# Gradient stage of a recurrent attention: rows' gradient for x rows only, 20 full row tiles, and transposes moved from TensorE to the DMA crossbar

## The chip, the cores and the metric

One core of one Trainium2 chip runs the whole program. The metric is the device time of one execution in microseconds, read for several executions. The profile is one execution with the hardware profiler on. Before the change the time is 5564.06 us (median of 3 runs, 5560.69 to 5575.1).

## The reference, cut to what matters

```python
def _A_ref(x, mem0, Wq, Wk, Wv, Wo, seg_len):       # x: (1, 2048, 640) bf16, after a layernorm
    ...                                              # H = 32 heads, Dh = 128, M = 8, seg_len = 32
    mem = mem0
    for s in range(n_seg):                           # 64 segments, one after the other
        xs = x[:, s * seg_len:(s + 1) * seg_len, :]
        h = jnp.concatenate([mem, xs], axis=1)       # 8 memory rows + 32 x rows
        q = jnp.einsum('btd,dhe->bhte', h, Wq)       # k and v alike
        ...
        p = _softmax(scores, axis=-1)
        o = jnp.einsum('bhqk,bhke->bhqe', p, v)
        o = jnp.einsum('bhte,hed->btd', o, Wo)
        mem = o[:, :M, :]
        outs.append(o[:, M:, :])
    return jnp.concatenate(outs, axis=1)
# out = x + _A_ref(xn) * silu(B_ref(xn)); returned: out and the gradients
# with respect to x, mem0, Wq, Wk, Wv, Wo, w1, w3, w2
```

The change concerns one stage of the backward pass. It has, in memory, the softmax probabilities P and the scores' gradient dS, and the rows of q, k and of the outputs' gradient. For each tile of 3 segments (96 x rows and 24 memory rows, 120 in all; 22 tiles cover 64 segments, the last with one segment) and for each four heads (512 columns; eight such groups) it makes the rows' gradients of v, k and q. From these come the gradients of Wv, Wk and Wq (a product over rows with the rows h) and the gradient of the rows of h (a product over columns with the weights).

## The kernel before

The stage, cut to the parts that the argument touches. `nc.tensor` is TensorE, `nc.sync` the queue of SyncE (SP), `nc.scalar` ScalarE (ACT), `nc.gpsimd` GpSimd (POOL), `nc.vector` VectorE (DVE). A "unit" is one tile of rows in one group of four heads.

```python
def ld(u):                                   # loads of one unit
    nc.sync.dma_start(dS[0:n, :, 0:n], k.DSR[tl][:, h0:h0 + 4, :])
    nc.sync.dma_start(Pr[0:n, :, 0:n], k.PR[tl][:, h0:h0 + 4, :])
    for nm_ in ("g", "q", "k"):
        ...
        k.load_x(r, nm, src, nc.scalar if nm_ == "g" else nc.sync)
        k.load_m(r, tl, nm_, c0, c0 + 512, nc.gpsimd)

def s1(u):                                   # turn dS on TensorE
    for j in range(4):
        nc.tensor.transpose(pt[:, j, :], dS[0:n, j, :], k.ident[0:n, 0:n])
    nc.vector.tensor_copy(dST[0:n, :, 0:n], pt[0:n])

def s2(u, i):                                # rows' gradient i: P, dS or turned dS times rows
    for j in range(4):
        nc.tensor.matmul(pr[:, j * P:(j + 1) * P], lh[0:n, j, :], rh[0:n, j * P:(j + 1) * P], start=True, stop=True)
    ...                                      # PSUM to gr: ACT, DVE, ACT for i = 0, 1, 2

def s3(u, i0, i1):                           # turn the gradients on TensorE, copy into a ring
    for i in range(i0, i1):
        for j in range(4):
            nc.tensor.transpose(pt[:, i - i0, j, :], st["g", u, i][0:n, j * P:(j + 1) * P], k.ident[0:n, 0:n])
    ...
    k.copy(ring[:, i0:i1, :, d0:d0 + p1 - p0], pt[:, :, :, p0:p1], eng='s' if c == 2 else 'v')

def s4(u):                                   # turned gradients times weights, windows of 128 rows
    for w in range((120 * tl) // P, (120 * tl + n) // P):
        for h in range(2):
            for i in range(3):
                for j in range(4):
                    nc.tensor.matmul(pg[:], ring[:, i, j, r0:r0 + P], Ws[qd][i][:, j, 320 * h:320 * h + 320], ...)
        ...                                  # DVE adds pg to the accumulator

def wg(qd, i):                               # weight gradient i of the group: 22 tiles x 5 products
    for tl in range(NTL):
        for dc in range(DC):
            nc.tensor.matmul(accs[dc][:], hr[0:n, tl, dc * P:(dc + 1) * P], st["g", NTL * qd + tl, i][0:n, :], ...)
    for dc in range(DC):
        ot = io.tile([P, 512], BF16, name="wgo", tag="wgo", bufs=4)
        k.copy(ot[:], accs[dc][:], eng='vs'[dc % 2])
        nc.sync.dma_start(outf[2 - i][dc * P:(dc + 1) * P, c0:c0 + 512], ot[:])

for qd in range(8):
    for tl in range(NTL):                    # "unit part": ld(u+4), s2(u+2), s1(u+3), s3(u+1), s4(u)
        ...
    ...                                      # weights and first three units of the next group are loaded
    for i in range(3):                       # "product part"
        wg(qd, i)
        if qd < 7:
            next(h)                          # first steps of the next group
```

## Time and profile before

| kernel before | value |
|---|---|
| median of 3 runs | 5564.06 us |
| span and mean granted TensorE clock of the profiled run | 5562.0 us, 0.952 |
| unit part / product part / whole group, mean of the last seven groups, from the starts of the products (a group is counted from one product part to the next, so the two parts do not quite add up to it) | 107.5 / 78.3 / 186.7 us |
| first unit part, from the first product | 120 us |

From the page of the kernel before: busy time of each engine in us (share of the span) and its instructions; then the busy tenths of TensorE in 40 equal slices, and the share of the DMA engines likewise.
```profile
PE 4935.7 (89%) x66673; PEld 3152.5 (57%) x67020; DVE 2343.2 (42%) x7398; ACT 1783.4 (32%) x4953; POOL 1570.4 (28%) x2604
...
PE   4987888888888677989999997999999999998999
...
DMA  7553455555555686666666666354335433657332
```
A slice is 139 us, so the stage lies in slices 25 to 36, and slices 26 to 35 are wholly in it. There TensorE stands at 9, and DMA between 3 and 6.

### The profile page before, as it was taken

To read this page: it belongs to the slowest core of one execution; us is meant where nothing else is said; L and a number is where in the kernel's file an instruction comes from. 1 tells how busy PE (TensorE), PEld (TensorE's weight loads), DVE (VectorE), ACT (ScalarE), POOL (GpSimd) and SP (SyncE) were. 2 spreads that over 40 slices of the span, in tenths; PEclk is the share of its full clock that TensorE was granted. 3 is DMA by queue.
4 is the path that set the end of the run, shared out by engine and by line. 5 is a ranking of instruction groups with operands and counts; after the bars stand their busy time and mean duration, and the time that the engine had idled before them with its cause. 6 is when DMAs were issued, how large, how long until landed. Compare 5 with 4: busy or idle time off the path is not lost. (4 is left out here: it accounts for less than half of the span.)

```text
span 5562.0 us, 164947 instructions
## 1 busy us (share of the span) xinstructions
PE 4935.7 (89%) x66673; PEld 3152.5 (57%) x67020; DVE 2343.2 (42%) x7398; ACT 1783.4 (32%) x4953; POOL 1570.4 (28%) x2604
## 2 busy tenths in 40 slices
PE   4987888888888677989999997999999999998999
PEld 2554555555555444656666665566556655666665
DVE  5833555555555323444444542233223322311451
ACT  2422555555555322323333332233113312300111
POOL 0000344444444212333333333243224322310000
PEclk9998999999999778999999998999999999999999
DMA  7553455555555686666666666354335433657332
GB/s 252 171 185 90 137 152 153 158 156 162 153 151 143 152 171 155 176 186 184 186 184 178 185 169 130 76 124 99 94 74 126 98 87 83 162 166 188 106 117 92
DMA packets 1126617, 808.27 MB, mean 145 GB/s; under 512 B 672971, under 2 KB 1016679, under 8 KB 1123179
## 3 DMA queue, kind: packets, MB, share of 16 engines
q1 hardware_dynamic: 884995, 555.06, 37.3%
q0 software_dynamic: 91472, 144.46, 9.3%
q10 hardware_dynamic: 149388, 98.17, 6.3%
q8 instruction: 529, 8.67, 0.7%
q14 instruction: 233, 1.91, 0.1%
HBM read 468.47 MB, written 296.78 MB: 138 GB/s over the span
## 5 line engine op out<-in xcount | busy, mean ns | idle before, releaser
L1403 PE MATMUL wg<-gr,hr 120*128 120x512 bf16 (+1 forms) x2640 | 592.9, 386 | 17.3 <-DVE dST L1335 13.1
L1381 PE MATMUL g<-w,gT 128*128 128x320 bf16 x3840 | 548.4, 299 | 0.0
L1403 PEld LDWEIGHTS <-hr 120*128 120x128 bf16 (+1 forms) x2640 | 258.9, 99 | 343.1 <-issue 52.1
L1381 PEld LDWEIGHTS <-gT 128*128 128x128 bf16 x3840 | 368.8, 98 | 136.3
L243 POOL DMA_DIRECT2D r<-GOS x256 | 143.4, 564 | 795.8 <-PE r6p L1345 704.8
L90 DVE CAST wgo<-wg 128x512 bf16<-128x512 f32 x72 | 47.5, 688 | 589.2 <-issue 281.8
L316 PEld LDWEIGHTS <-hx 128*32 128x32 bf16 x7680 | 179.7, 97 | 169.4 <-issue 12.4
L90 DVE CAST stg<-bank 128x512 bf16<-128x512 f32 x256 | 177.0, 692 | 208.4 <-PE bank L316 199.4
L335 PEld LDWEIGHTS <-gkv 128*8 128x8 bf16 x8192 | 189.7, 87 | 107.4 <-DVE gkv L1012 23.8
L619 ACT ACTIVATE xP<-xsp,xnm 120x120 bf16<-120x120 f32 (+1 forms) x704 | 240.5, 376 | 8.5 <-DVE xnm L615 4.5
L1390 DVE TENSOR_TENSOR ghacc<-ghacc,g 128x320 f32<-128x320 f32 x240 | 117.0, 487 | 277.7 <-PE g L1381 277.7
L92 ACT CAST wgo<-wg 128x512 bf16<-128x512 f32 x48 | 25.8, 589 | 640.3 <-PE wg L1403 640.3
L1163 POOL DMA_DIRECT2D DSR<-gdS x176 | 101.6, 577 | 426.5 <-DVE gdS L1161 383.3
L1348 ACT CAST gr<-r6p 120x512 bf16<-120x512 f32 (+1 forms) x176 | 103.3, 587 | 361.7 <-PE r6p L1345 340.8
L668 POOL DMA_DIRECT2D OR<-xv x163 | 94.6, 580 | 418.9 <-ACT xv L667 287.0
L92 ACT COPY gT<-t6g 128x960 bf16<-128x960 bf16 (+5 forms) x216 | 167.0, 792 | 119.9 <-PE t6g L1364 117.0
L630 POOL TENSOR_TENSOR xP<-xP,xrz 120x480 bf16<-120x480 bf16 x163 | 161.8, 992 | 141.0 <-ACT xP L619 96.5
L1161 DVE SCALAR_TENSOR_TENSOR gdS<-gdp,Dx,gPr 120x120 bf16<-120x120 f32 (+1 forms) x680 | 182.7, 330 | 0.0
L1232 PE MATMUL gbank<-WqT,ident 128*128 128x512 bf16 x453 | 159.5, 402 | 20.1 <-issue 12.2
L335 PE MATMUL bank<-Wo,oTm 128*32 128x320 bf16 x4032 | 177.0, 329 | 0.1
L316 PE MATMUL gbank<-WoT,gox 128*32 128x512 bf16 x2560 | 153.6, 387 | 24.6 <-POOL gox L967 21.2
L1364 PE MATMUL t6g<-ident,gr 120*128 120x120 bf16 (+1 forms) x2112 | 172.0, 221 | 3.3 <-DVE wgo L90 2.7
(339 smaller groups left out, 10991.0 us busy)
## 6 DMA issues: line engine op xcount, KB each, us to landing
QVS<-stg SPq DMA_DIRECT2D x128, 256.0 KB
gqv<-QVS SPq DMA_DIRECT2D x108, 192.0 KB
vTt<-VTD SPq DMA_DIRECT2D x64, 320.0 KB
VTD<-gvT POOLq DMA_DIRECT2D x168, 120.0 KB, 3.6
OR<-xv POOLq DMA_DIRECT2D x163, 120.0 KB, 2.5
DSR<-gdS POOLq DMA_DIRECT2D x168, 112.5 KB, 3.4
dS<-DSR SPq DMA_DIRECT2D x168, 112.5 KB
P<-PR SPq DMA_DIRECT2D x168, 112.5 KB
```

Source lines behind the costliest of these rows:

```text
L90: return nc.vector.tensor_copy(out, in_)
L92: return nc.scalar.copy(out, in_)
L243: eng.dma_start(d, src if src.shape[0] > 1 else src[0])
L316: k.nc.tensor.matmul(bank[32 * g:32 * g + 32, :], x[:, dc, :], W[:, dc, c0:c0 + 512], start=(dc == 0), stop=(dc == k.DC - 1), tile_positio ...
L335: k.nc.tensor.matmul(pm[p0:p0 + nq, 0:320], x[:, h, :], W[:, h, 320 * b:320 * b + 320], start=(first and i == 0), stop=(last and i == 15), ...
L619: nc.scalar.activation(Pb[0:n, j, 0:n], sp[0:n, j, :], ACT.Exp, bias=nmx[0:n, j:j + 1], scale=k.scale, accum_out=Z[0:n, j:j + 1])
L630: eng.tensor_tensor(Pb[0:n, :, 0:n], Pb[0:n, :, 0:n], bc_last(rz[0:n], n), ALU.mult)
L1161: nc.vector.scalar_tensor_tensor(dS[0:n, j, :], dp[0:n, j, :], Dx[0:n, j:j + 1], Pr[0:n, j, :], op0=ALU.subtract, op1=ALU.mult)
L1232: nc.tensor.matmul((bA if g in ("W1", "G1", "G2") else bB)[:], k.ident[:], WqT[:, 0, 0:512], start=True, stop=True)
L1364: nc.tensor.transpose(pt[:, i - i0, j, :], st["g", u, i][0:n, j * P:(j + 1) * P], k.ident[0:n, 0:n])
L1381: nc.tensor.matmul(pg[:], ring[:, i, j, r0:r0 + P], Ws[qd][i][:, j, 320 * h:320 * h + 320], start=(i == 0 and j == 0), stop=(i == 2 and j ...
L1403: nc.tensor.matmul(accs[dc][:], hr[0:n, tl, dc * P:(dc + 1) * P], st["g", NTL * qd + tl, i][0:n, :], start=(tl == 0), stop=(tl == NTL - 1))
```

## The change

The intent is to take work from TensorE, which bounds the stage. (1) The gradient of h is made for x rows only, as the memory rows' one isn't used: x rows now come first in a tile, so that 16 windows of 128 rows stand in for 20. (2) Two of the 22 tiles are handled first, written to memory, and read back into the eight free partitions of the 20 others, so that the weight gradients need 20 tiles of 128 rows. (3) dS and the gradients are turned by two crossbar transposes of the DMA per unit, issued by SP, in place of sixteen TensorE transposes and three copies. (4) The loads of x rows are all issued by ScalarE; the loads of dS and P become contiguous; five buffers replace three.

The core of the diff, with cuts; the rest changes the layout of the tiles elsewhere (x rows first).
```diff
-            nc.sync.dma_start(dS[0:n, :, 0:n], k.DSR[tl][:, h0:h0 + 4, :])
-            nc.sync.dma_start(Pr[0:n, :, 0:n], k.PR[tl][:, h0:h0 + 4, :])
+            nc.sync.dma_start(dS[0:n], k.DSR[tl][:, h0:h0 + 4, :])
+            nc.sync.dma_start(Pr[0:n], k.PR[tl][:, h0:h0 + 4, :])
 ...
-                k.load_x(r, nm, src, nc.scalar if nm_ == "g" else nc.sync)
+                k.load_x(r, 0, src, nc.scalar)
 ...
+        def dturn(u):
+            dST = io.tile([P, 4, P], BF16, name="dST6", tag="dST6", bufs=4)
+            turned_load(k, dST[:], st["l", u][0][:].rearrange("p j c -> p (j c)"))   # SP: DMA transpose
 ...
+            g3 = gra[:, tl] if tl < NF else gp.tile([120, 3, 512], BF16, name="grs", tag="grs", bufs=2)[:]
 ...
+            if tl >= NF:
+                nc.gpsimd.dma_start(k.GSP[qd, r0:r0 + n], g3[0:n])
+
+        def spill(qd):
+            nc.gpsimd.dma_start(gra[120:P], k.GSP[qd].rearrange("(t r) i c -> r t i c", r=8))
 ...
-                    nc.tensor.transpose(pt[:, i - i0, j, :], st["g", u, i][0:n, j * P:(j + 1) * P], k.ident[0:n, 0:n])
+            turned_load(k, ring[:, :, a:a + nx], st.pop(("g", u))[0:nx].rearrange("p i c -> p (i c)"))
 ...
-            for tl in range(NTL):
-                n = k.geo(tl)[3]
+            for tl in range(NF):                     # NF = 20
 ...
+            for p in range(NTL):
+                u = u0 + p
+                if p + 3 < NTL:
+                    s2(u + 3)
+                    ld_to(u + 3 + NB)                # NB = 5
+                dturn(u + 4)
+                if p + 2 < NTL:
+                    s3(u + 2)
                 s4(u)
+                if p == 4:
+                    spill(qd)
```

## The prediction

> **What bounds the kernel now.** I read the page first (TensorE busy 89% of the span, at 8 or 9 tenths in nearly every slice, so the kernel is bound by TensorE almost everywhere), then the source lines of the changed stage in the view of one line's instructions, which says when each starts. The weight gradient stage runs from 3410 us (first transpose of dS) to 4915 us (last product), 1505 us. It handles eight groups of four heads. In each a "unit part" makes the rows' gradients of 22 row tiles, turns them and multiplies them with the weights (22 iterations), and a "product part" forms the weight gradients from all 22 tiles. The busy times by window, for the second group's two parts and the whole stage (columns: window, length, busy us and instructions of PE, PEld, DVE, ACT, POOL, then granted clock, DMA share, GB/s):
> ```profile
> 3610.00:3719.00 109.00, 103.29 (x1081) 81.34 (x1080) 50.91 (x113) 44.53 (x71) 55.84 (x101) 0.97 0.53 124
> 3719.00:3797.00 78.00, 74.00 (x351) 33.32 (x350) 6.16 (x11) 3.23 (x6) 1.70 (x3) 0.98 0.27 60
> 3410.00:4915.00 1505.00, 1414.16 (x11408) 916.27 (x11408) 458.14 (x992) 382.68 (x616) 457.64 (x828) 0.96 0.43 103
> ```
> One group takes 109 + 78 = 187 us, and eight of them 1496 us. TensorE is busy 94% of it; the transfers are at half share in the unit part and a quarter in the product part. Everything but TensorE has slack. The groups of instructions in the stage say what fills TensorE:
> ```profile
> L1403 PE MATMUL wg<-gr,hr 120*128 120x512 bf16 x2520 | 564.6, 386 | 17.3 <-DVE dST L1335 13.1 <-DVE gr L1350 2.6 <-DVE ghacc L1388 0.6
> L1381 PE MATMUL g<-w,gT 128*128 128x320 bf16 x3840 | 548.4, 299 | 0.0
> L1364 PE MATMUL t6g<-ident,gr 120*128 120x120 bf16 x2016 | 168.3, 223 | 3.3 <-DVE wgo L90 2.7 <-ACT wgo L92 0.5
> L1333 PE MATMUL t<-ident,dS 120*128 120x120 bf16 x672 | 67.4, 227 | 42.7 <-DMA dS<-DSR 39.0 <-DVE wgo L90 2.1 <-DVE gr L1350 0.8
> ```
> The reader is to see that the idle time (third field) is near zero, and that transposes by TensorE (L1364, L1333) are a real part of the load. Durations overlap in the pipeline, so one instruction's cost comes from the starts in the timeline of one iteration:
> ```profile
> 3663.45 0.37 PE L1333 MATMUL t<-ident,dS 120*128 120x120 bf16 x4
> 3663.66 0.58 PE L1364 MATMUL t6g<-ident,gr 120*128 120x120 bf16 x8
> 3664.08 0.39 PE L1345 MATMUL r6p<-r,dST 120*128 120x128 bf16 x4
> 3664.30 0.37 PE L1364 MATMUL t6g<-ident,gr 120*128 120x120 bf16 x4
> 3664.51 3.42 PE L1381 MATMUL g<-w,gT 128*128 128x320 bf16 x24
> 3667.78 0.39 PE L1345 MATMUL r6p<-r,P 120*128 120x128 bf16 x4
> ```
> Four small ones pass every 0.21 to 0.22 us (55 ns each), and 24 of 320 columns in 3.27 us (136 ns each). A weight product costs 592.9 us / 2640 = 225 ns, from the page.
>
> [...] from 3420 to 3428 us, where the three weight transposes run nearly alone, 242 GB/s move at a DMA share of 1.16.
> ```profile
> 3420.00:3428.00 8.00, 0.04 (x1) 0.00 (x0) 0.00 (x0) 0.60 (x1) 0.56 (x1) 0.50 1.16 242
> 3630.00:3690.00 60.00, 60.00 (x660) 48.56 (x658) 30.84 (x70) 26.84 (x43) 32.70 (x59) 1.00 0.60 142
> L280 SPq DMA_TRANSPOSE w<-in_A_Wv_dram x8: 2285/2478/3046, 3418.6 to 4652.2; - x8
> L280 SPq DMA_TRANSPOSE x<-in_B_w_dram x4: 1210/4666/15807, 5091.1 to 5117.4; - x4
> ```
> I use the measured rate. No transpose in this trace has SBUF as its source, as all the new ones do.
>
> **The change, part by part.** Removed from TensorE: all turns of dS (704) and of the gradients (2112), 2816 x 55 ns = 155 us. Rows' gradients for x rows only: 16 windows of 128 rows in place of 20, so 8 x 4 x 24 = 768 matmuls x 136 ns = 105 us. Twenty full tiles of 128 rows in place of 22 of 120 (the two leftover tiles, 160 rows, go through memory into the eight free partitions of each of the 20): 240 x 225 ns = 54 us. Sum **314 us**, all on the path, as TensorE has no other work to do there. If nothing else came to bind, the stage would take 1191 us and the kernel 5250.
>
> Also removed, off the path: DVE's 176 copies of turned dS (0.4 us) and the copies of turned gradients by ACT and DVE (about 0.96 and 0.41 us per unit). DVE and ACT are under half busy, so this gains nothing directly.
>
> Added, per unit: a crossbar transpose of dS, 128 x 512 elements (131 KB), and one of the three gradients, 96 x 1536 (295 KB), both on SP's queue. Moved: q and k loads from SP to ACT. The dS and P rows become 1024 contiguous bytes in place of four of 240; the packet records give 73 ns for 1024 bytes and 18 for 240, the same rate, so I book no gain.
>
> New TensorE time of a group: unit part 19 x 12 x 55 ns (three units' worth moves to the product part) + 16 windows x 3.27 = 12.5 + 52.3 = 65 us; product part 300 x 225 ns + 3 x 0.66 = 69.5 us. Now the other resources in the unit part:
> - Transfers. 19 units are loaded there (five buffers let the others go ahead). A unit's loads are 5 x 123 = 614 KB: 11.7 MB. Transposes: 22 x 131 + 20 x 295 KB = 8.8 MB. Output rows and the leftover tiles' reads and writes: about 1.8 MB. Sum 22.3 MB. The second row above gives 142 GB/s at share 0.60, 237 GB/s at full share: **94 us**, against 65 of TensorE.
> - SP's issue. A transpose of 640 rows x 128 took at least 1.21 us to issue, one of 640 x 512 about 2.4: a line through these gives 1.14 us for the dS one and 1.51 for the gradients' (estimates). With two plain issues of 0.45 us: 3.55 us x 19 + 2.65 x 3 = **75 us**, without waits.
> - The loop through SP. The built program issues a unit's dS and P loads when TensorE has freed their buffer, then the dS transpose for the next step, which TensorE needs one iteration later. Issue of both loads 0.9 us, of the transpose 1.1, landing some 2 us behind its queue, the last product 0.3: about 4.3 us, x 22 = **95 us**. And every transfer of SP and ACT waits for the one eight issues before, seven per unit, so about one unit's transfers are in flight.
>
> So the stage turns from TensorE-bound to transfer-bound in its unit part: I take 95 us, and 69 for the product part, whose transfers (outputs, next weights, three units' loads, near 30 us) are hidden. A group falls from 187 to 164 us, eight save 184; 5 us back for a start that waits on more loads before the first product. **5564 - 179 = 5385 us.** Outside the stage only layouts change (x rows first, memory rows last), with the same instruction counts; I book nothing.
>
> **The rivals.**
> (a) TensorE stays the bound: transposes out of SBUF run faster than those out of HBM[...]. For: stores out of SBUF in the packet records run at some 20 GB/s per engine against 14 for loads. Against: three limits of 75 to 95 us all lie above 65. It would give 5250 to 5290.
> (b) Transposes out of SBUF cost SP far more: [...] they block the queue's loads behind them. For: the 640 x 1664 one took 8 to 16 us to issue. At 3 us for the gradients' one, SP needs about 105 us and the group 175: 5470 and above; at 5 us the change loses.
> (c) The stalls cool TensorE's clock: in 3410 to 3533 us, where it waited, the clock was 0.90. If the unit part ran at 0.8, its work would be 79 us, still under 95; little added.
> (d) The leftover tiles' round trip through memory delays the product part. It is written in the previous product part and read at the fifth iteration, some 60 us before use: hidden.
>
> **Range and chances.** The unit part may take 80 us (5265) to 107 us (5485). I say 5270 to 5480. Two per cent is 5453, a unit part of 103 us or less: 0.75 faster, 0.21 within, 0.04 slower.
>
> **What would show it.** Right: in the stage 2400 and 3072 matmuls in place of 2640 and 3840, no TensorE transposes; TensorE idle in the unit part before the products with P or dST, ended by a transfer; DMA share near 1 there; product part about 69 us, DMA share low. SP's transposes at 1.1 and 1.5 us with SP occupied most of the unit part. Wrong: TensorE over 90% busy in the unit part (rival a), or SP's transposes of several us (rival b), or stages before 3400 us shifted by over 20 us.

## The result, and the profile after

| | before | after |
|---|---|---|
| median (lowest to highest), 4 runs each of the same rounds | 5568.7 us (5560.69 to 5575.1) | 5715.53 us (5697.27 to 5738.35) |
| ratio, 95% interval | | 1.0266 (1.0226 to 1.0307): slower |
| span, mean granted clock of the profiled run | 5562.0 us, 0.952 | 5711.4 us, 0.923 |
| unit part / product part / group, mean of the last seven | 107.5 / 78.3 / 186.7 us | 128.5 / 71.8 / 201.4 us |
| first unit part | 120 us | 161 us |

A ratio here is the mean time of one kernel's runs over the mean of the other's of the same rounds, so it is not quite the ratio of the medians. Experiments ran in several sessions, in which the kernel before took medians from 5557 to 5569 us. So where two of them are compared, I take the difference of their ratios times 5560 us (one per cent is 56 us); the medians differ by up to 10 us more. The changed kernel's own ratio is known to 0.4%, or 23 us, and every difference from it carries that much.

The page of the kernel after, the same rows as before.
```profile
PE 4724.6 (83%) x62801; PEld 2940.6 (51%) x63196; DVE 2185.0 (38%) x6934; ACT 1619.9 (28%) x4737; POOL 1537.9 (27%) x2627
...
PE   4987888888888758899999984776787678699999
...
DMA  7552555555554785667666649689769877857332
```
The removed work is gone (211 us of busy time), yet the program is longer. A slice is now 143 us. In slices 26 to 35 TensorE has fallen from 9 to between 6 and 8 tenths, and DMA has risen to between 6 and 9.

First, did the time come from the stage? The first 3390 us, first of the kernel before, then after (window, length, then busy us and instructions of PE, PEld, DVE, ACT, POOL, granted clock, DMA share, GB/s).
```profile
0.00:3390.00 3390.00, 2908.26 (x50747) 1832.01 (x51093) 1686.55 (x5939) 1324.98 (x4197) 1051.74 (x1692) 0.94 0.60 165
```
```profile
0.00:3390.00 3390.00, 2908.13 (x50515) 1825.77 (x50863) 1681.40 (x5920) 1323.79 (x4192) 1001.55 (x1686) 0.94 0.59 166
...
3872.00:3998.00 126.00, 80.90 (x623) 56.40 (x622) 31.61 (x58) 22.78 (x42) 51.70 (x93) 0.82 1.12 185
3998.00:4067.00 69.00, 66.89 (x323) 31.05 (x328) 6.19 (x10) 4.68 (x9) 7.74 (x14) 1.00 0.32 78
3428.00:5066.00 1638.00, 1191.71 (x7536) 704.47 (x7583) 300.80 (x535) 218.46 (x400) 472.39 (x851) 0.87 0.82 146
```
Everything before the stage does the same work as it did. The stage, from its first product to its last, grew from 1498 us (3414.2 to 4912.3) to 1636 us (3428.2 to 5063.7), and began 14 us later; that is the whole difference. The 14 us belong to this execution and not to the change: the last product into `bank`, long before the stage, starts at 1856 us here, at 1840 us in the kernel before, and at 1836 to 1842 us in e1, e10 and e14, which share everything up to there with the changed kernel. The second and third line after are one group. Its product part is short, as hoped. In its unit part TensorE is busy 81 of 126 us, at a clock of 0.82, while the DMA share is over 1 with only 185 GB/s moved: 23.3 MB.

The groups of instructions in the stage after (busy us, mean ns of one, idle before them and what ended it), and from the waits of the stage after (total us, times, longest) what TensorE waited for.
```profile
L1379 PE MATMUL g<-w,ghacc 128*128 128x320 bf16 x3072 | 528.6, 338 | 34.1 <-DMA ghacc<-gr 33.6
L1400 PE MATMUL wg<-gr,hr 128*128 128x512 bf16 x2352 | 531.4, 385 | 20.3 <-DVE grs L1351 14.0
```
```profile
PEld L1345 <- DMA dST<-dS: 372.7, 90, 17.0
...
PE r6p L1345 <- DMA dST<-dS: 331.1, 84, 12.8
```
The counts are the expected ones (2352 records of 2400; some are missing from a trace). A product with the weights (L1379) now counts 528.6 / 3072 = 172 ns against 143 before, with the granted clock at 0.82 in the unit part above, against 0.97 in one of the kernel before (3610 to 3719 us). The turned dS, made by a transfer, is what TensorE waits for: 331 us in all. But a wait on a transfer can mean full DMA engines, or one late transfer, or a late issue. The last is answered by the issue times of SP's transposes (ns min/median/max) in the kernel after:
```profile
L272 SPq DMA_TRANSPOSE dST<-dS x176: 1188/1194/7958, 3422.4 to 4984.2; - x176
...
L272 SPq DMA_TRANSPOSE ghacc<-gr x160: 1252/1344/5356, 3470.5 to 4989.6; - x160
```
1.19 and 1.34 us, where 1.14 and 1.51 were estimated: a transpose out of SBUF is cheap to issue.

Two spots in the trace stood out. **The burst.** At the fifth iteration of a group the leftover tiles' rows are read back: 491.5 KB into partitions 120 to 127. The windows around it in one group, then the landing time of that transfer over the eight groups (min/median/max).
```profile
4088.00:4096.00 8.00, 5.84 (x43) 4.12 (x44) 1.25 (x3) 1.26 (x3) 3.59 (x7) 0.79 1.24 237
4096.00:4106.00 10.00, 3.58 (x32) 2.57 (x29) 2.00 (x4) 0.91 (x2) 3.56 (x7) 0.86 1.11 83
```
```profile
DMA to landing us min/median/max: 13.1/14.4/15.0
```
For 10 us all transfers together fall from 237 to 83 GB/s, while the share stays above 1. The next step of TensorE sits idle 11.41 us for the turned dS:
```profile
4110.99 0.61 PE L1345 MATMUL r6p<-r,dST 120*128 120x128 bf16 x4 [11.41 <-DMA dST<-dS]
```
**The cold start.** SP's queue in the product part of one group after (start, length, what, count), and its main wait over the program.
```profile
3801.48 4.09 SPq L272 DMA_TRANSPOSE w<-in_A_Wq_dram  x1
3819.40 29.95 SPq L1405 DMA_DIRECT2D out_dram<-wgo  x10
3849.77 0.34 SPq L1312 DMA_DIRECT2D dS<-DSR  x1
...
3852.68 1.62 SPq L272 DMA_TRANSPOSE ghacc<-grs  x1
```
```profile
SPq L1405 <- DVE wgo L90: 451.4, 47, 24.2
```
SP stands in front of each output until the product part has made it, 451 us in all, and behind that output in the same queue stand the next units' loads and transposes. In the last 10 us or so of that product part (3860 to 3870 us) 9 GB/s move. The next unit part then begins with everything to load.

### The profile page after: what moved, and what is told of

It reads as the page before.

```text
span 5711.4 us, 156769 instructions
## 1 busy us (share of the span) xinstructions
PE 4724.6 (83%) x62801; PEld 2940.6 (51%) x63196; DVE 2185.0 (38%) x6934; ACT 1619.9 (28%) x4737; POOL 1537.9 (27%) x2627
## 5 line engine op out<-in xcount | busy, mean ns | idle before, releaser
L1379 PE MATMUL g<-w,ghacc 128*128 128x320 bf16 x3072 | 528.6, 338 | 34.1 <-DMA ghacc<-gr 33.6
L1400 PE MATMUL wg<-gr,hr 128*128 128x512 bf16 x2352 | 531.4, 385 | 20.3 <-DVE grs L1351 14.0
L1379 PEld LDWEIGHTS <-ghacc 128*128 128x128 bf16 x3072 | 334.1, 111 | 199.5 <-DMA ghacc<-gr 35.0
L1400 PEld LDWEIGHTS <-hr 128*128 128x128 bf16 x2400 | 237.4, 99 | 307.4 <-issue 36.8
L1345 PE MATMUL r6p<-r,dST 120*128 120x128 bf16 (+1 forms) x704 | 77.8, 240 | 365.2 <-DMA dST<-dS 331.1
L1388 DVE TENSOR_TENSOR ghacc<-ghacc,g 128x320 f32<-128x320 f32 x192 | 93.7, 488 | 523.8 <-PE g L1379 523.8
L1349 ACT CAST gr<-r6p 120x512 bf16<-120x512 f32 x160 | 93.8, 587 | 649.2 <-PE r6p L1345 293.4
L1345 PEld LDWEIGHTS <-dST 120*128 120x128 bf16 (+1 forms) x704 | 48.3, 105 | 382.1 <-DMA dST<-dS 372.7
L245 POOL DMA_DIRECT2D r<-KS x256 | 141.2, 554 | 158.8 <-PE r6p L1345 119.7
L308 PE MATMUL gbank<-WoT,gox 128*32 128x512 bf16 x2560 | 154.6, 388 | 25.6 <-POOL gox L957 22.3
```

Of the source, the lines that this page charges most:

```text
L245: eng.dma_start(d, src if src.shape[0] > 1 else src[0])
L308: k.nc.tensor.matmul(bank[32 * g:32 * g + 32, :], x[:, dc, :], W[:, dc, c0:c0 + 512], start=(dc == 0), stop=(dc == k.DC - 1), tile_positio ...
L1345: nc.tensor.matmul(pr[:, j * P:(j + 1) * P], lhs[i][0:n, j, :], rw[i][0:n, j * P:(j + 1) * P], start=True, stop=True)
L1379: nc.tensor.matmul(pg[:], ring[:, 4 * i + j, r0:r0 + P], Ws[qd][i][:, j, 320 * h:320 * h + 320], start=(i == 0 and j == 0), stop=(i == 2 a ...
L1400: nc.tensor.matmul(accs[dc][:], hr[:, tl, dc * P:(dc + 1) * P], gra[:, tl, i, :], start=(tl == 0), stop=(tl == NF - 1))
```

## The experiments

The theories, with the letters that the expectations use: **A**, the DMA engines are full in the unit part, with the burst as an extra; **B**, waits: the loop through SP is too slow, and a late turned dS holds TensorE; **C**, the cooled clock; **D**, moving the row loads to ScalarE delays its evictions or the loads; **E**, the cold start. All were timed in three rounds or more; "ratio" is against the kernel before (1.0266 is the changed kernel).

### The burst: e2_nospill, e14_after_split

e2 leaves the read of the leftover tiles out (zeros stand in the eight partitions). It is wrong: the three weight gradients are off by 0.25.
```diff
-                if p == 4:
-                    spill(qd)
```

> Wrong weight gradients on purpose: the leftover tiles' rows are not brought into the eight free partitions of the 20 tiles (those are zeroed once). Theory A, the transfers bind in the unit part and the transfer into eight partitions slows all others for about 10 us per group: the kernel falls from 5715 by about 80 us to 5635, and the iteration after the fifth loses its 10 to 15 us. Rival B, a chain of waits through SP (loads, then the dS transpose issued one iteration before its use) sets the pace: under 15 us gained. Rival C, the cooled clock sets the pace: nothing gained beyond 15 us.

Measured: 5632.56 us, ratio 1.0133 (1.0110 to 1.0156): 74 us less. A unit part of e2:
```profile
3850.00:3961.00 111.00, 78.51 (x624) 55.49 (x623) 31.55 (x58) 22.73 (x42) 51.06 (x92) 0.85 1.14 205
```
So the burst costs about 9 us per group. The unit part shown is the fastest of e2's; over seven groups its rate is 192 GB/s, against 182 in the changed kernel (bytes and times of the unit parts in the two traces). A share of 1.14 at about 200 GB/s is still far from the 237 GB/s of the prediction.

e14 keeps the result right and moves the same bytes in 20 pieces of 24.6 KB, one per iteration.
```diff
-        def spill(qd):
-            nc.gpsimd.dma_start(gra[120:P], k.GSP[qd].rearrange("(t r) i c -> r t i c", r=8))
+        def spill(qd, t):
+            nc.gpsimd.dma_start(gra[120:P, t], k.GSP[qd, 8 * t:8 * t + 8])
 ...
-                if p == 4:
-                    spill(qd)
+                if p >= 2:
+                    spill(qd, p - 2)
```

> The changed kernel with nothing but that transfer cut into 20 of 24 KB. If it is the burst into eight partitions that holds all the engines: nearly the 83 us of the run without it, 5640 to 5660. If it is the bytes into these partitions at any time: unchanged, 5700 or more, as the engines are full all the time.

Measured: 5640.49 us, ratio 1.0144 (1.0120 to 1.0169): 68 us less, nearly all that leaving the bytes out gave. So the loss was not in the bytes but in sending them at once to eight partitions.

### The late dS: e1_ahead

The turn of dS is issued one iteration earlier.
```diff
-                dturn(u + 4)
+                if u + 5 < u0 + NTL + 4 and u + 5 < len(units):
+                    dturn(u + 5)                     # and dturn(u0 + 4) once per group
```

> Both crossbar transposes stay; the dS transpose of a unit is issued two iterations before its use in place of one (and its fifth unit's already during the product part). Same transfers, same packets. A (engines of the transfers full, crossbar packets the bulk of it): within 25 us of 5715. B (latency of the dS transpose, loads and transposes issued in a row by SP): TensorE's wait for the turned dS mostly goes, unit part 105 us or less, kernel 5560 or less.

Measured: 5686.42 us, ratio 1.0228 (1.0198 to 1.0258): 21 us less by the ratios, 29 by the medians. The interval overlaps the changed kernel's, so the size is uncertain. B wanted more than five times that. The wait itself went, as B expected: these are TensorE's longest waits in e1's stage.
```profile
PE g L1379 <- DMA ghacc<-gr: 124.7, 56, 9.3
PE r6p L1345 <- ACT gr L1349: 104.2, 37, 7.6
PE r6p L1345 <- DMA dST<-dS: 66.1, 17, 9.2
```
The 331 us for turned dS have become 66, but the waits for turned gradients rose from 34 to 125 us and those for ScalarE's evictions (`ACT gr`) from 4 to 104. A wait that goes and leaves the time nearly as it was did not set the pace; something behind it did.

### The cold start: e6_outs

The outputs' stores are issued after the next units' loads; two more output buffers hold them.
```diff
-                nc.sync.dma_start(outf[2 - i][dc * P:(dc + 1) * P, c0:c0 + 512], ot[:])
+                outs.append((outf[2 - i][dc * P:(dc + 1) * P, c0:c0 + 512], ot[:]))
 ...
-                wg(qd, i)
+                outs = wg(qd, i)
                 if qd < 7:
                     next(h)
+                for o in outs:
+                    nc.sync.dma_start(*o)
```

> In the product part SP issues the next units' loads and transposes ahead of the outputs, which wait for TensorE (two more output buffers). E (cold start: in the product part SP stands before the outputs 450 us in all, transfers run at share 0.3, and the first unit-part iterations wait 9.5 us for loads that could have been there): 8 to 10 us less per group, kernel 5640 to 5655. A in its plain form (the engines of the transfers are full for the whole unit part whatever the start): part of the loads is out of the unit part, but only one unit more: within 30 us of 5715.

Measured: 5644.36 us, ratio 1.0145 (1.0130 to 1.0160): 67 us less, as E said. But the edit does two things, the new order and six output buffers in place of four, and the profile doesn't put the gain where E has it. Of the 6.6 us that a group became shorter (201.4 to 194.8), the unit part gave 2.3 and the product part the rest. Over the stage TensorE's waits for copies into output buffers (`DVE wgo`) fell from 21 to 6 us and those for evictions behind them (`DVE grs`) from 14 to 3.5. So e6 shows what both are worth together; the cold start alone was not isolated.

### Is it bytes? e8_R2

The gradients' crossbar transpose is done twice, the second time into a buffer that nobody reads. Nothing waits for it, so a theory of waits alone has little to charge it with.
```diff
+            turned_load(k, twice[:, :, 0:nx], g3)      # unread
```

> Every crossbar transpose of the gradients is issued twice, the second time into a buffer that nobody reads: the cost of one kind of transfer, measured by itself. A, at the 29.6 ns that a 256-byte packet takes on average in the trace: 23040 packets per group, 43 engine-us over 1.12: 38 us per group more, kernel 6020; at the undisturbed 18 ns: 23 us per group, 5900. B or any theory in which waits and not transfers set the pace (SP's own issue grows by 27 us per group, to 102 of 128 us): under 60 us more, 5775.

Measured: 5899.59 us, ratio 1.0608 (1.0591 to 1.0625): 190 us more. The mean unit part rose from 128.5 to 153.7 us, 25.2 us for 20 x 295 KB = 5.9 MB: 234 GB/s. A unit part of e8:
```profile
3905.00:4057.00 152.00, 85.09 (x624) 58.01 (x623) 31.49 (x58) 23.73 (x42) 51.54 (x93) 0.78 1.16 193
```
This is the second value that A named, with a packet at 18 ns; the first, with the mean of 29.6 ns, was off by 120 us. A rival has to be answered: the second transposes also cost SP 20 x 1.34 = 27 us of issue per group, as much as the unit part grew. e10 below answers it. It adds two loads per unit to SP's queue (0.33 and 0.36 us, some 14 us per group, 110 in all) and costs 13 us. So SP's issue time is not a likely cause (e10 also takes work from ScalarE, so this is not proof), and it is the bytes, though nobody needs them, that lengthen the stage by about their own time: A holds in the unit part.

### Three losses together, and what is left: e15_three, e16_warm

e15 is the changed kernel with the split burst, the outputs after the loads, and dS turned ahead.

> The changed kernel with both crossbar transposes kept and three remedies at once: the transfer into eight partitions cut in 20, outputs after the next units' loads, dS transposes one iteration earlier. If the three losses are separate: 5715 - 75 - 71 - 29 = 5540, a group of 179 us, the unit part about 110 us with the transfers' share still above 1.1. If they were one slack counted three times: 5600 or more.

Measured: 5572.81 us (20 runs), ratio 1.0027 (1.0017 to 1.0037): 133 us less than the changed kernel, where the three alone gave 68 + 67 + 21 = 156. It lies between the two expectations; the losses are mostly separate. The profiles, one of each, give a second reading without what happens before the stage: from first product to last it is 52 us shorter in e14, 48 in e6 and 23 in e1, 123 together, and 124 in e15. Now a unit part of e15, the longest of seven, and TensorE's longest waits in its stage:
```profile
3822.00:3944.00 122.00, 82.39 (x629) 56.77 (x628) 31.70 (x58) 22.75 (x42) 61.60 (x112) 0.83 1.15 187
```
```profile
PE r6p L1345 <- ACT gr L1349: 131.0, 52, 7.4
PE g L1379 <- DMA ghacc<-gr: 93.5, 56, 4.9
PE r6p L1345 <- DMA dST<-dS: 69.0, 22, 8.4
```
With all three known losses undone the kernel is no faster than the one before. The share is still above 1, at 187 GB/s, and the mean unit part of the last seven groups is 115.6 us (22.8 MB, 197 GB/s). The longest wait is now for ScalarE's evictions, and ScalarE stands before them mostly until a transfer lands (idle 640 us before L1349, of which 165 until `dST<-dS`, 98 until `r<-QVS` and 72 until `r<-KS`), with the row loads in its own queue. Theory D was tested in the changed kernel only (e10 below), where TensorE's wait for dS (331 us in all) may have hidden it; e15 with the q and k loads on SP was not run.

Is it the clock, at 0.83? e16 keeps TensorE busy in its waits with four filler products of 512 columns per unit.
```diff
+                for _ in range(4 if i == 2 else 0):
+                    nc.tensor.matmul(pr[:], lhs[0][0:n, 0, :], rw[0][0:n, :], start=True, stop=True)
```

> The same with four filler products of 512 columns ahead of each product with the turned dS, where TensorE waits; they only keep its clock up (0.9 us of work per unit at full clock). A: the transfers set the pace, clock up from about 0.85 to 0.95 in the unit part, time within 25 us of the run without the fillers. C (the cooled clock holds part of the unit part): 40 us or more faster.

Measured: 5609.62 us, ratio 1.0085 (1.0070 to 1.0100). A unit part of e16:
```profile
4020.00:4140.00 120.00, 94.09 (x707) 62.64 (x706) 31.87 (x58) 22.93 (x42) 61.52 (x112) 0.93 1.13 190
```
The clock rose to 0.93 here (0.88 to 0.93 in the windows that I read), and the kernel became 32 us slower. C finds no support: a higher clock shortened nothing. The run isn't a clean one, as the fillers are work too (TensorE is busy 94 us here, 82 in e15). But in e15 TensorE is idle for 40 of 122 us, which a slow clock doesn't explain.

### Which part of the change costs: e3_dsT_pe, e4_grT_pe, e5_both_pe, e10_sp, e7_22

e3 turns only dS on TensorE again, e4 only the gradients, e5 both; all else stays as changed.
```diff
-            turned_load(k, dST[:], st["l", u][0][:].rearrange("p j c -> p (j c)"))          # e3, e5
+            for j in range(4):
+                nc.tensor.transpose(pt[:, j, :], dS[0:n, j, :], k.ident[0:n, 0:n])
+            nc.vector.tensor_copy(dST[0:n, :, 0:n], pt[0:n])
 ...
-            turned_load(k, ring[:, :, a:a + nx], ...)                                       # e4, e5
+            for i0, i1 in ((0, 2), (2, 3)):
 ...
+                        nc.tensor.transpose(pt[:, 4 * (i - i0) + j, :], g3[0:nx, i, j * P:(j + 1) * P], k.ident[0:nx, 0:nx])
+                k.copy(ring[:, 4 * i0:4 * i1, a:a + nx], pt[:], eng='s' if i0 == 0 else 'v')
```

> Only the dS transposes go back to TensorE; the gradients stay on the crossbar. A: dS transposes are a third of the crossbar packets, some 21 of 141 engine-us per group; the unit part falls from 126 to about 107 us, the kernel to about 5565, TensorE now waiting for the gradients' transposes. B: the wait for the turned dS was the pace; with it gone the unit part falls to about 100 us or less, the kernel to 5515 or less.

Measured: 5565.74 us, ratio 1.0008 (0.9981 to 1.0034): 143 us less, as A expected.

> Only the gradients' transposes go back to TensorE; dS stays on the crossbar. A: two thirds of the crossbar packets go, about 43 engine-us of 141 per group: unit part about 88 us, kernel about 5415. B: the chain through the dS transpose is untouched, TensorE still waits for the turned dS: unit part 118 us or more, kernel 5660 or more.

Measured: 5625.29 us, ratio 1.0127 (1.0106 to 1.0148): a miss for both theories. It takes 5.9 MB of 23 out of a group's unit part and gives 77 us. The burst, the cold start and the late dS were still in that kernel, and I had booked none of them; that led to e14 and e6.

> Both kinds of transposes back on TensorE; x rows only, 20 full tiles and the loads by ScalarE stay. A and B: TensorE bound again, 105 + 54 us less of it than in the kernel before: about 5410, DMA share about 0.6 in the unit part. If the fold into eight partitions costs also here, about 10 us per group more: 5490.

Measured: 5480.88 us, ratio 0.9857 (0.9837 to 0.9877), near the second of the two values named, as if the burst still cost its 10 us per group. That it is the burst alone is not shown. In e5 TensorE also waits 71 us for ScalarE's copies of turned gradients (`ACT ghacc`), with ScalarE's row loads in the same queue; in e13 below, which cuts the burst and gives q and k back to SP, 11 us. The two were not separated.

e10 gives the loads of q and k back to SP.
```diff
-                k.load_x(r, 0, src, nc.scalar)
+                k.load_x(r, 0, src, nc.scalar if nm_ == "g" else nc.sync)
```

> Loads of q and k rows issued by SP as in the kernel before; only the g rows stay with ScalarE. A: transfers bind, who issues them does not matter, or SP's own issue (3.55 + 0.85 us per iteration) becomes a second bound: 5715 to 5800. D (ScalarE stands in its own issue waits, 220 us in the trace, and its evictions behind them hold TensorE up): 5660 or less.

Measured: 5725.22 us, ratio 1.0290 (1.0264 to 1.0316), the same as the changed kernel within the intervals. D falls for the changed kernel.

e7 undoes the fold into full tiles: 22 tiles of 120 rows, no round trip. The buffers didn't all fit, so it has three output buffers in place of four.
```diff
-            for tl in range(NF):
+            for tl in order:
+                n = k.geo(tl)[3]
 ...
-                ot = io.tile([P, 512], BF16, name="wgo", tag="wgo", bufs=4)
+                ot = io.tile([P, 512], BF16, name="wgo", tag="wgo", bufs=3)
 ...
-                if p == 4:
-                    spill(qd)
```

> The fold is undone: 22 tiles of 120 rows in the weight products, no round trip through memory into eight partitions (the output buffers go from 4 to 3 to make room). The dummy-free form of the run without the spill: 83 us gained there, 240 products of 225 ns = 54 us paid back, so about 5685. If the fold's transfer was not the cause but the missing data dependence was: 5740 or more.

Measured: 5732.78 us, ratio 1.0305 (1.0279 to 1.0332): a miss. The unit part fell by 8 us as without the burst, but the product part rose by 13.4 us instead of 6.75. The three output buffers are a second change in it: ACT now waits for outputs to leave too (44 us; only DVE did before). That this is the 6.7 us more was not tested. So e7 doesn't measure the fold.

### Toward a better version: e9_best, e13_split, e18_best2

e9 turns everything on TensorE, gives q and k back to SP, and has 22 tiles with three output buffers. It was the guess before e14.

> A version that should beat both: x rows only, all transposes on TensorE, no fold (22 tiles), q and k row loads issued by SP. By the sum for TensorE it saves the 105 us of the four windows per group against the kernel before; it had 5557 in the last rounds, so 5452, if TensorE is bound as before. If ScalarE's issue waits and the fold are not what holds the run with both kinds of transposes on TensorE at 5481, then it is at 5481 plus 54 less 80 = 5455 as well or above; more telling is the wait of ScalarE for row loads (141 us there), which should go to under 40 us.

Measured: 5487.89 us, ratio 0.9871 (0.9842 to 0.9899), 36 us over the expectation: unit part 89.3 us, but product part 83.6; it has the three output buffers too.

e13 keeps the 20 full tiles and cuts the burst as e14 does, with all turns on TensorE and q and k on SP.

> A version that should beat both: x rows only, both kinds of transposes on TensorE, q and k loads issued by SP, and the fold kept but its transfer into eight partitions cut into 20 of 24 KB, one per iteration. By the sum: the unit part 89 us as in the run without the fold, the product part 72 us as in the runs with it, 161 a group: about 5375. If cutting does not help, the unit part is at 97 us or more: 5440 or more.

Measured: 5384.1 us, ratio 0.9681 (0.9657 to 0.9706): better than both kernels.

e18 is e13 with the outputs after the next units' loads, as in e6.

> The faster version (5384) with the outputs after the next units' loads. There the transfers have slack and the unit part starts only about 2 us late: 5350 to 5390; if the cold start costs there what it costs in the changed kernel, 5320 or less.

Measured: 5333.49 us (5332.08 to 5337.16), ratio 0.9592 (0.9577 to 0.9606): the fastest, 49 us under e13, between the two expectations. A unit part of e18:
```profile
3762.00:3848.00 86.00, 81.93 (x963) 66.36 (x963) 44.49 (x100) 37.17 (x62) 61.38 (x112) 1.00 0.59 163
```
TensorE is busy 82 of 86 us at full clock. It is its bound again, with the window and tile savings in and no crossbar turn.

### Do crossbar turns pay once everything else is right? e19_dsT_xbar, e20_grT_xbar

e19 is e18 with dS turned on the crossbar, ahead as in e1. In e18 the DMA share is 0.59, so there seems to be room.

> The fastest version (5333) with the dS transposes on the crossbar, issued two iterations ahead. TensorE loses 39 us in all; the transfers gain 11264 packets of 256 bytes per group, 13 us at 18 ns over 16 engines, on a unit part of 86 us whose share is about 0.6, so they still fit: 5300 to 5335 if transfers only bind when full. If a crossbar transfer costs waits at half load as well: 5345 or more.

Measured: 5391.49 us, ratio 0.9684 (0.9659 to 0.9708): 51 us slower than e18. A unit part of e19, and from the view of the tile of turned dS who waited for it (us, times):
```profile
3775.00:3866.00 91.00, 80.93 (x879) 63.86 (x877) 38.66 (x79) 38.37 (x63) 61.50 (x112) 0.96 1.04 184
```
```profile
  PEld L1345: 69.6, 25
  PE r6p L1345: 55.7, 23
```
The share went from 0.59 to 1.04, 1.04 x 91 - 0.59 x 86 = 44 us of all engines, for 184 x 91 - 163 x 86 = 2.7 MB more in the unit part. At 237 GB/s 2.7 MB are 11.5 us. TensorE waits again for a turned dS.

e20 is e18 with the gradients turned on the crossbar instead, and the row loads by ScalarE.

> The fastest version with the gradients' transposes on the crossbar (row loads by ScalarE, as SP has the long transposes to issue). TensorE loses some 100 us in all; the transfers gain 23 us per group as measured by the doubled run, on about 55 us of engine time: share near 0.95 in a unit part of 80 us. Full engines again: 5400 or more, as the run with only the dS turn on TensorE had 5566 before the two remedies worth 146; if they just fit, 5300.

Measured: 5459.9 us, ratio 0.9814 (0.9789 to 0.9838): 123 us slower than e18. Not all of that need be the crossbar: in e20's stage TensorE waits 67 us for turned gradients, but 95 us for ScalarE's evictions (`ACT gr`), which share a queue with the row loads moved there. e19 is the clean comparison. No version tried here gained from either turn, alone or together.

## Why the prediction was wrong

**What held.** TensorE's work in the stage fell as counted: 3072 products with the weights, 2352 recorded of 2400 for the weight gradients, no transposes. The product part was put at 69.5 us; it measured 71.8, and 67.8 in e15. SP's transposes were estimated at 1.14 and 1.51 us of issue and took 1.19 and 1.34, so rival (b) falls. TensorE waits for turned dS (331 us) at a DMA share above 1 (1.12 in the unit part above), so the stage did become transfer-bound, and rival (a) falls. Rival (c), the clock, found no support in e16. Nothing outside the stage moved with the change.

**The step that failed is the transfer time of the unit part.** The text says "142 GB/s at share 0.60, 237 GB/s at full share: 94 us", and from it a unit part of 95 us. It measured 128.5. The bytes were nearly right (22.3 MB predicted, 23.3 measured); the rate was not: 185 GB/s. The miss is 5716 - 5385 = 331 us. The runs divide it so:

1. **Rival (d) was dismissed as "hidden".** The prediction asked when the leftover tiles would be needed and found 60 us of slack. It didn't ask what the read does to the transfers beside it. Split into pieces the read gives 68 us back (e14), left out 74 (e2). The packet records of the changed kernel put the read at 8.4 to 9.6 us over the eight groups, 51 to 59 GB/s for its 491.5 KB. That the other transfers stall meanwhile is what the 83 GB/s show; that their packets stand behind it in the same engines is argued, not shown.
2. **The cold start** was not in the text. It has "whose transfers (...) are hidden" for the product part, but in SP's order the next units' loads stood behind outputs that did not exist yet. The new order and two more output buffers gave 67 us together (e6); how much of it is the cold start stays open.
3. **The late dS** is 21 us (e1). The loop through SP had been put at 95 us, level with the transfers; it is a small term.

Together 1 to 3 are worth 143 us by the medians (5715.5 - 5572.8, e15), which leaves 188 of 331.

4. **The rate itself.** In e15 the mean unit part is 115.6 us instead of 95: 7 x 20.6 = 144 us. The first unit part was booked at 120 - 12.5 + 5 = 112.5 us and took 160: 47 us more. It moved 30 MB in the changed kernel (161 us at 186 GB/s), with h and all first loads among them; I did not divide it further. The product parts give 8 x 1.7 = 14 back. That is 177 of 188 us.

Why was the rate wrong? The scaling from a half-loaded engine to a full one assumed that packets last as long in the new mix as in the old one. The packet records say otherwise. Before, from 3630 to 3690 us, a 1024-byte load packet of SP took 55 ns on average (median 46), and from 3719 to 3735 us a 256-byte crossbar packet of the weights 21.4 (median 18). After, from 3872 to 3998 us, 1024-byte loads took 89 ns (those issued by ACT) and 67 (by SP), and the 34,688 crossbar packets 29.6 ns, with a median of still 18. So most crossbar packets are as fast as before, but 1398 of them (4%) last over 60 ns and hold 36% of their time, 66 of them over 1 us each. The burst is not the reason: in the unit part of e15 shown above, with the burst cut, it is 1545 of 33,792 with 37% of the time. The prediction also took 73 ns for 1024 bytes out of its records; that is the mean at the start of a product part (3719 to 3735 us), and in the unit part the median is 46.

e8 shows that added crossbar bytes lengthen the unit part at 234 GB/s, nearly the rate that the prediction used, while the unit parts shown with crossbar turns move 184 to 205 GB/s in all, and the weight transposes nearly alone 242 in the kernel before. It is therefore the mix that is slow, not each added transpose in it. e19 shows the same from the other side: the first crossbar transposes among ordinary loads took 44 us of all engines for 2.7 MB. **What stays open** is what holds the slow packets: neither their cause nor why ordinary loads beside them stretch was isolated. A run with the crossbar alone in the engines would have needed another order of the whole stage.

The sum was thus right in what it took off TensorE and wrong in the price of what it put in its place. Turning on TensorE costs, by the prediction's own 55 ns, 155 us of the program, and the crossbar costs more than that: e15, the best version with both crossbar turns, is 242 us slower than e18 (which also has q and k loads on SP). The two other savings, 105 and 54 us by the prediction, do pay: e18 has both, and its gain over the kernel before is 4.1%, or 227 us, with the outputs' order in it too.

## What to carry to other kernels

Here a DMA share of 0.6 was not 0.4 of free capacity at the rate of the moment (from e18 to e19 it went from 0.59 to 1.04 for 2.7 MB more in the unit part), and a share above 1 did not tell the rate (1.11 with 83 GB/s, 1.12 with 185, 1.24 with 237): before work is moved from a bound engine to the transfers, measure the new kind of transfer among the ones that are there. A large transfer into a few partitions (491.5 KB into eight) held up all others here while it ran (83 GB/s in all for 10 us, from 237), however late its data were needed, and cost little when cut into 20 pieces (e14 gives back 68 of the 74 us). When a wait is removed and the time stays, as in e1, look for what the engine waits for next before calling it the cause. Change one thing per run: e6, e7 and e20 each changed two, and none of them settles its question alone.
